# Which heads ScalarE's score pair takes, and one first pass over two PSUM banks on VectorE

## The chip, the cores and the metric

The kernel runs on one core of a Trainium2 chip. A core has five engines with instruction queues of their own: TensorE (PE in the profile; PEld is its weight load), VectorE (DVE), ScalarE (ACT), GpSimd (POOL) and SyncE (SP), which issues most DMAs. The metric is the device time of one execution in microseconds, as the median of several runs. Before the change it is 758.08 us, the median of 6 runs between 755.37 and 759.51.

## The reference

Two independent branches are computed from two inputs of 2048 rows and 640 columns, and their results stand side by side in the output.

```python
# A: spectral filter
X = rfft2(x);  y = irfft2(X * (w_r + 1j * w_i))           # to bf16
# B: attention, 32 heads of width 20
q, k, v = split(x @ wqkv)
p = softmax(q @ k.T * 20 ** -0.5)                         # 2048 x 2048 for each head
y = (p @ v) @ wo
out = concatenate([A, B], axis=-1)
```

The softmax has 32 x 2048 x 2048 exponentials. They are the bulk of the work outside TensorE.

## The kernel before, in words

**Units and tiles.** The attention is cut into 32 units. A unit is one block of 512 queries (`qc`) for a group `g` of four heads. The four heads sit on four groups of 32 partitions, so that their score matmuls use four separate row groups of TensorE. A unit has 16 key tiles `kt` of 128 keys, and for each key tile four heads `j` (0 to 3): 64 score tiles of 128 x 512, 2048 in all. A score tile is one matmul (`score_mm`, line 816) into one PSUM bank.

**Two ways to an exponential.** ScalarE takes two tiles at once. They lie in banks 0 and 1, or in 2 and 3, by turns; one activation of 128 x 1024 (`try_exp`, line 1413) writes their exponentials in f16 into a ring of 14 slots, that is seven pairs. VectorE takes the four heads of one key tile, a quad, and approximates the exponential by integer arithmetic. Each of the four tiles gets a first pass out of its PSUM bank into a quarter of a buffer `Ib` (`dve_fill`, line 950). When all four are there, two more passes over 2048 columns follow (lines 992 and 993), and a small scaling of V (line 1000). There are two buffers, hence at most two quads under way.

**PV.** A wave of four matmuls, one for each head of one key tile (`try_pv`, line 1071), multiplies exponentials with V. A key tile of ScalarE's needs one wave and a quad of VectorE's needs three, since its approximation is a sum of three parts. A wave is issued only when all four heads of the key tile are there. With eight tiles waiting (`VMIN`) the planner issues two waves together, under pressure from the ring also one.

**Banks.** Banks 4 to 7 (`POOLB`) are for everything but ScalarE's pairs: VectorE's tiles, the PV sum of the unit, and the jobs of projections, of the filter branch and of the output.

**The order.** The order of every engine's instructions is written when the kernel is built, by a planner (`run`) that keeps a time for each engine, a cost for each instruction and the moment from which each result is visible. It takes steps as engines come free: `try_exp` for ScalarE, `pick_dve` for VectorE, `step_pe` for TensorE. The latter first tries `try_act_fill`, then PV waves, then a job of the other branch, then a fill for VectorE alone (`try_dve_fill`), and at last a filler matmul [...] (line 1502). Nothing is decided at run time; the chip only keeps the order on each engine and the waits between engines.

**Picking.** `try_act_fill` needs a free pair of banks. `pick_set` fills ScalarE's pair with two tiles of different heads: first from `aq`, the open tiles of a key tile that ScalarE has begun, then from the next key tile. `pick_dve_tile` offers a tile for the same group of matmuls from `dq`, the open tiles of VectorE's quad, if its head isn't among those of the group:

```python
for t in self.dq:
    if t[2] not in bad_j and all(t[2] != d[0][2] for d in dts):
        return t
```

`dve_wants` allows it while VectorE's queued work is under 2.0 us (1.6 us with 0.6 us counted for a second tile), and while fewer than three of the four banks are held by others than PV. `free_bank` takes the lowest free bank of `POOLB`. At most three first passes are in flight (`MAXD`).

Of the kernel before, what the change touches and what calls it, by code (L numbers as in the profile page):

```python
# [297 lines left out]
class KB:  # L298
# [449 lines left out]
    def start_attention(self):  # L748
        self.rem = [[(kt, j) for kt in range(16) for j in range(4)] for _ in range(NU)]
        self.ua = 0  # L750
        self.qs = [list(range(16)) for _ in range(NU)]
        self.aq = []
        self.dq = []
        self.grp = 0
        self.sets = []
        self.act_started = False
        self.pn = 0
        self.dbatch = 0
        self.dtiles = []
        self.dfly = 0  # L760
        self.batches_open = {}
        self.bat = {}
        self.pv = []
        self.upv = 0
        self.pv_bank = {}
        self.pv_started = {}
        self.pv_left = [64] * NU
        self.units_done = 0
        self.act_tiles = 0
        self.dve_tiles = 0  # L770
        self.alias_done = set()
# [80 lines left out]
    DMIN = 14  # L852
    DMIN_LAST = 12

    def free_bank(self):
        for b in self.POOLB:
            if self.bank_owner[b] is None and self.P.peek("pe", w=[("ps", b)]) <= self.now:
                return b
        return None
# [4 lines left out]
    def try_act_fill(self):  # L864
        if self.ua >= NU:
            return False
        banks = self.SETS[self.grp]
        if any(self.bank_owner[b] is not None for b in banks):
            return False
        if len(self.sets) >= 2:  # L870
            return False
        if self.P.peek("pe", w=[("ps", b) for b in banks]) > self.now:
            return False
        tiles = self.pick_set(len(banks))
        if not tiles:
            return False
        left = sum(4 * len(q) for q in self.qs[self.ua:self.ua + 2]) + len(self.aq)
        if len(tiles) < len(banks) and left > len(tiles) and self.act_started and not self.starved():
            return False
        for t in tiles:  # L880
            self.take_tile(t)
        bl = banks[:len(tiles)]
        rk = set()
        for u, kt, j in tiles:
            rk.update(self.kq_keys(u, kt))
        dts = []
        while len(tiles) + len(dts) < 4 and self.dve_wants(len(dts)):
            db = self.free_bank()
            if db is None:
                break  # L890
            dt = self.pick_dve_tile(set(t[2] for t in tiles), dts)
            if dt is None:
                break
            dts.append((dt, db))
            self.dve_take(dt, db)
        wk = [("ps", b) for b in bl]

        def fn(e):
            inst = None
            for (u, kt, j), b in zip(tiles, bl):  # L900
                inst = self.score_mm(e, u, kt, j, b)
            return inst
        n = len(tiles)
        self.put("pe", fn, 216.0 + 4.0 * (n - 1), r=list(rk), w=wk, name="fillA", mode="S")
        for b in bl:
            self.bank_owner[b] = "act"
        self.sets.append((tiles, bl, self.grp))
        self.grp ^= 1
        self.act_started = True
        self.act_tiles += n  # L910
        for dt, db in dts:
            self.dve_fill(dt, db, 4.0)
        return True

    def starved(self):
# [20 lines left out]
        self.dfly += 1  # L936
        self.dve_tiles += 1

    def dve_fill(self, t, bank, occ):
        u, kt, j = t  # L940
        self.put("pe", lambda e: self.score_mm(e, u, kt, j, bank), occ, r=self.kq_keys(u, kt), w=[("ps", bank)], name="fillD", mode="S")
        b = self.dbatch % 2
        i = len(self.dtiles)
        self.dtiles.append(t)
        I16_ = self.Ib[b].bitcast(I16)
        o = I16_[:, i * 512:(i + 1) * 512]
        in_ = self.ps[:, bank, :]

        def fn(e, en):
            return e.tensor_scalar(o, in_, 0.0, 31744.0, ALU.max, ALU.min)  # L950
        al = self.first("xn3", ("xz", 3)) if b == 1 else []

        bt = self.bat.setdefault(self.dbatch, [0, None])

        def done():
            self.bank_owner[bank] = None
            self.dfly -= 1
            bt[0] += 1
            if bt[1] is not None and bt[0] == bt[1][0]:
                bt[1][1]()  # L960
        self.dve_push([(fn, 604.0, [("ps", bank)], [("I", b, i)] + al, [], "p1")], done)
        if len(self.dtiles) == 4:
            self.close_batch()

# [492 lines left out]
    def try_dve_fill(self, room):  # L1457
        if not self.act_started or self.ua >= NU or room < 216.0 + (2 if self.mode != "S" else 1) * self.SW or self.dve_backlog() > self.DVE_LOW:
            return False
        dts = []  # L1460
        used = set()
        while len(dts) < 2 and self.dve_wants(len(dts)):
            db = self.free_bank()
            if db is None:
                break
            dt = self.pick_dve_tile(used, dts)
            if dt is None:
                break
            dts.append((dt, db))
            self.dve_take(dt, db)  # L1470
        for i, (dt, db) in enumerate(dts):
            self.dve_fill(dt, db, 216.0 if i == 0 else 4.0)
        self.nown += len(dts)
        return bool(dts)

# [752 lines left out]
```

## Time and profile before

| | us |
|---|---|
| median of 6 runs | 758.08 |
| the profiled execution | 756.85 |
| its span, first to last instruction | 755.0 |
| ScalarE busy (784 of 797 instructions are exponentials) | 729.5 |
| VectorE busy | 672.4 |
| TensorE busy, its ends modelled | 723.5 |
| GpSimd busy | 133.5 |

A row of groups reads: line, engine and operation, what is written and read with its size, how often, then total busy time and mean length in ns, then the engine's idle time just before these instructions and what ended it. Successive instructions of one engine overlap a little: the exponentials are 1.120 us long by the row and start 0.904 us apart (the median). A line of the timeline reads: start, length, engine, line, operation, how many instructions it merges, and in brackets the idle time before it and who ended that.

### The profile page before, as it was taken

The numbers are of one execution on the slowest core, as the hardware profiler recorded it, in microseconds if no ns is written. First come the engines' busy times: TensorE is split into PE (matmuls) and PEld (weight loads), VectorE is DVE, ScalarE is ACT, GpSimd is POOL, SyncE is SP. The second block draws the span as 40 slices with busy tenths as digits, with TensorE's granted clock in tenths as the row PEclk, the third lists the DMA queues.
The fourth block names the chain that finished last, engine by engine and source line by source line (L and its number), as shares of the span: only waits on it lengthen the run. The fifth ranks groups of instructions, "written<-read, shape, count | busy, mean of one in ns | idle before, by whom it ended". The sixth has DMA issues, their size and how long they took to land.

```text
span 755.0 us, 16333 instructions
## 1 busy us (share of the span) xinstructions
PE 723.5 (96%) x6488; PEld 231.7 (31%) x6537; DVE 672.4 (89%) x1259; ACT 729.5 (97%) x797; POOL 133.5 (18%) x141
## 2 busy tenths in 40 slices
PE   8999999999999999999999999999999999999997
PEld 4422332423322222232233333322322333333233
DVE  3599999989899998999998899999898998898995
ACT  5899999999999999999999999999999999999995
POOL 7398740000000100003020022000000000000000
PEclk9999999999999999999999999999999999999999
DMA  9022321102012126113020121130010211111101
GB/s 307 26 68 89 104 95 40 44 8 62 21 38 55 49 78 205 43 47 116 19 52 7 56 54 35 36 98 22 20 47 19 88 36 55 39 52 43 43 13 38
DMA packets 43502, 44.66 MB, mean 59 GB/s; under 512 B 16740, under 2 KB 36582, under 8 KB 43166
## 3 DMA queue, kind: packets, MB, share of 16 engines
q1 hardware_dynamic: 42654, 42.25, 19.0%
q0 software_dynamic: 768, 1.32, 0.7%
q8 instruction: 53, 0.87, 0.5%
q14 instruction: 27, 0.22, 0.1%
HBM read 28.47 MB, written 8.36 MB: 49 GB/s over the span
## 4 chain that ended last, share of the span: by engine, by line
ACT 68%; PE 23%; DVE 8%; issue 1%; DVEq 0%
ACT arena L1413 67%; PE ps L816 8%; PE ps L1071 5%; DVE arena L950 3%; PE ps L1821 2%; PE ps L649 2%; PE ps L698 2%; PE ps L620 1%; PE ps L1217 1%; DVE arena L993 1%; DVE arena L992 1%; DVE arena L1853 1%; DVE arena L1000 1%; PE ps L1977 1%; PE ps L578 1%
## 5 line engine op out<-in xcount | busy, mean ns | idle before, releaser
L1413 ACT ACTIVATE arena<-ps 128x1024 f16<-128x1024 f32 x784 | 722.3, 1120 | 8.5 <-PE ps L816 7.2
L950 DVE TENSOR_SCALAR arena<-ps 128x512 int16<-128x512 f32 x480 | 320.3, 682 | 32.8 <-PE ps L816 29.5
L816 PE MATMUL ps<-arena 32*128 32x512 bf16 x2048 | 308.9, 385 | 12.7 <-ACT arena L1413 8.5
L1071 PE MATMUL ps<-arena 128*32 128x512 f16 x3008 | 235.7, 385 | 1.9 <-DVE arena L1000 1.0
L816 PEld LDWEIGHTS ps<-arena 32*128 32x128 bf16 x2048 | 76.0, 91 | 292.2 <-ACT arena L1413 270.6
L1123 POOL TENSOR_TENSOR arena<-arena 128x512 bf16<-128x512 f32 x30 | 41.3, 1376 | 510.2 <-DMA arena<-rd 510.2
L992 DVE TENSOR_SCALAR arena<-arena 128x2048 int16<-128x2048 int16 x120 | 88.5, 738 | 3.8 <-PE ps L1071 3.4
L993 DVE TENSOR_SCALAR arena<-arena 128x2048 int16<-128x2048 int16 x120 | 86.2, 718 | 0.6
L1071 PEld LDWEIGHTS ps<-arena 128*32 128x32 bf16 x3008 | 50.9, 94 | 96.0 <-issue 64.3
L649 PE MATMUL ps<-arena 128*128 128x512 bf16 x148 | 44.4, 383 | 2.7 <-issue 1.9
L1821 PE MATMUL ps<-arena 128*128 128x322 bf16 (+1 forms) x198 | 38.2, 304 | 0.8 <-DVE arena L950 0.6
L1977 PE MATMUL ps<-arena 128*128 128x320 bf16 (+1 forms) x192 | 35.7, 302 | 0.0
L698 PE MATMUL ps<-arena 128*128 128x160 bf16 x320 | 31.5, 234 | 1.3 <-DVE arena L950 0.5
L1853 DVE TENSOR_TENSOR arena<-ps,arena 128x644 bf16<-128x644 f32 (+1 forms) x34 | 27.9, 821 | 3.2 <-PE ps L1821 2.8
L1925 PE MATMUL ps<-arena 128*128 128x512 bf16 (+3 forms) x122 | 29.2, 332 | 1.5 <-issue 1.4
L1000 DVE TENSOR_SCALAR arena<-arena 128x96 bf16<-128x96 bf16 x120 | 29.8, 249 | 0.0
L1217 PE MATMUL ps<-arena 128*128 128x320 bf16 (+1 forms) x152 | 28.8, 302 | 0.6 <-DVE arena L950 0.6
L698 PEld LDWEIGHTS ps<-arena 128*128 128x128 bf16 x320 | 21.3, 98 | 14.5 <-issue 9.8
L1102 DVE COPY arena<-ps 128x512 f32<-128x512 f32 (+1 forms) x33 | 21.9, 667 | 2.6 <-PE ps L1071 2.5
L661 DVE TENSOR_SCALAR arena<-ps 128x512 bf16<-128x512 f32 x34 | 23.2, 681 | 0.7 <-PE ps L649 0.6
L1738 PE MATMUL ps<-arena 128*128 128x512 bf16 x70 | 21.4, 383 | 1.6 <-issue 1.3
L704 DVE CAST arena<-ps 128x320 bf16<-128x320 f32 x32 | 15.5, 486 | 7.4 <-PE ps L698 7.2
(82 smaller groups left out, 367.9 us busy)
## 6 DMA issues: line engine op xcount, KB each, us to landing
arena<-rd SPq DMA_DIRECT2D x120, 64.0 KB
out_dram<-arena SPq DMA_DIRECT2D x32, 160.0 KB
arena<-in_A_x_dram SPq DMA_DIRECT2D x16, 160.0 KB
xs<-arena SPq DMA_DIRECT2D x16, 160.0 KB
arena<-xs SPq DMA_DIRECT2D x4, 640.0 KB
arena<-arena SPq DMA_DIRECT2D x105, 20.0 KB
arena<-ct SPq DMA_DIRECT2D x2, 1024.0 KB
arena<-ct SPq DMA_DIRECT2D x4, 512.0 KB
```

The lines of the kernel that those rows point to most:

```text
L649: return lambda e: e.matmul(o, l, r_, start=(cc == 0), stop=(cc == 4))
L698: return lambda e: e.matmul(o, l, r_, start=st, stop=(c == 4), skip_group_check=True)
L816: return e.matmul(self.ps[:, bank, :], self.KT[32 * j:32 * j + 32, g, kt * 128:(kt + 1) * 128], self.QT[32 * j:32 * j + 32, g, qc * 512:(q ...
L950: return e.tensor_scalar(o, in_, 0.0, 31744.0, ALU.max, ALU.min)
L992: self.dve_push([(lambda e, en: e.tensor_scalar(Ii, Ii, SH2, 0.0, ALU.subtract, ALU.max), occ, ik + pk, ik, [], "p3")], lambda: push(self. ...
L993: ops = [(lambda e, en: e.tensor_scalar(Gi, Ii, SH1, 0.0, ALU.subtract, ALU.max), occ, ik, [("G", b)], [], "p2")]
L1000: self.dve_push([(lambda e, en: e.tensor_scalar(vs, vi, W1, None, ALU.mult), 105.0, [("V", g // 2, kt), ("Vone",), ("Vpad",)], vk, [], "vs ...
L1071: inst = e.matmul(self.ps[32 * j:32 * j + 32, bank, :], v_, p_, start=s_, stop=False, tile_position=(0, 32 * j), skip_group_check=True)
L1123: self.pool_op(lambda e: e.tensor_tensor(on, of, bc, ALU.mult), 1600.0, r=pk + [("bcu", u, j) for j in range(4)] + [("bc", j) for j in ran ...
L1413: self.put("act", lambda e: e.activation(o, in_, AF.Exp, bias=ACT_BIAS, scale=ACT_SCALE), 0.8333 * 512 * n + 60.0, r=[("ps", b) for b in b ...
L1821: return lambda e: e.matmul(o, lhs, r_, start=st, stop=sp)
L1977: return lambda e: e.matmul(o, l, r_, start=(n == 0), stop=(n == 5))
```

## The change

The diff has two parts. In `try_act_fill`, after ScalarE's pair was picked in the old way, and if VectorE's quad has open tiles (`dq`) and VectorE wants work, the pair is picked again with the heads of the first two open tiles excluded, or else the head of the first. The new pair is used if it is complete and if it and the open tiles of ScalarE belong to at most two key tiles together. The second part concerns fills that carry two tiles for VectorE. `free_bank` gets an argument and prefers a bank that has a free neighbour, or, for the second tile, one that lies beside the first. If the two banks are neighbours, the first `dve_fill` only issues its matmul and notes itself in `half`; the second one pushes a single first pass of 128 x 1024 over both banks, with a planned cost of 1137 in place of 2 x 604. Both banks are given back when this pass is done. `try_dve_fill` gets the same treatment.

```diff
+    def free_bank(self, near=None):
+        bs = self.POOLB
+        if near is not None:
+            ok = [b for b in bs if self.bank_owner[b] is None and self.P.peek("pe", w=[("ps", b)]) <= self.now]
+            bs = sorted(bs, key=lambda b: not any(abs(b - c) == 1 for c in (near or ok)))
+        for b in bs:
...
         tiles = self.pick_set(len(banks))
         if not tiles:
             return False
+        if self.dq and self.dve_wants(0):
+            for k in (2, 1):
+                alt = self.pick_set(len(banks), [t[2] for t in self.dq[:k]])
+                if len(alt) == len(banks) and len({t[:2] for t in self.aq + alt}) <= 2:
+                    tiles = alt
+                    break
...
-            db = self.free_bank()
+            db = self.free_bank([d[1] for d in dts])
...
-        for dt, db in dts:
-            self.dve_fill(dt, db, 4.0)
+        if len(dts) == 2 and abs(dts[0][1] - dts[1][1]) == 1:
+            if dts[0][1] > dts[1][1]:
+                dts = [(dts[0][0], dts[1][1]), (dts[1][0], dts[0][1])]
+            self.dve_fill(dts[0][0], dts[0][1], 4.0, True)
+            self.dve_fill(dts[1][0], dts[1][1], 4.0)
+        else:
+            for dt, db in dts:
+                self.dve_fill(dt, db, 4.0)
...
-    def dve_fill(self, t, bank, occ):
+    def dve_fill(self, t, bank, occ, first=False):
...
-        in_ = self.ps[:, bank, :]
+        half = self.half
+        self.half = (i, bank) if first else None
+        banks = [bank] if half is None else [half[1], bank]
+        i0 = i + 1 - len(banks)
...
+        o = I16_[:, i0 * 512:(i + 1) * 512]
+        in_ = self.ps[:, banks[0]:bank + 1, :].rearrange("p b n -> p (b n)")
...
+        if not first:
+            self.dve_push([(fn, 604.0 if half is None else 1137.0, [("ps", b_) for b_ in banks], [("I", b, i0 + q) for q in range(len(banks))] + al, [], "p1")], done)
```

More of the change, by code (lines that the diff above doesn't have):

```diff
@@ L758, in start_attention @@
         self.dbatch = 0
+        self.half = None
         self.dtiles = []
@@ L853 @@
     DMIN_LAST = 12
-    def free_bank(self):
-        for b in self.POOLB:
+    def free_bank(self, near=None):
[4 more added lines that the diff above has]
+        for b in bs:
             if self.bank_owner[b] is None and self.P.peek("pe", w=[("ps", b)]) <= self.now:
@@ L945, in dve_fill @@
         I16_ = self.Ib[b].bitcast(I16)
-        o = I16_[:, i * 512:(i + 1) * 512]
-        in_ = self.ps[:, bank, :]
+        half = self.half
+        self.half = (i, bank) if first else None
+        banks = [bank] if half is None else [half[1], bank]
+        i0 = i + 1 - len(banks)
+        assert half is None or half == (i - 1, bank - 1)
+        o = I16_[:, i0 * 512:(i + 1) * 512]
+        in_ = self.ps[:, banks[0]:bank + 1, :].rearrange("p b n -> p (b n)")
         def fn(e, en):
@@ L955, in done @@
         def done():
-            self.bank_owner[bank] = None
-            self.dfly -= 1
-            bt[0] += 1
+            for b_ in banks:
+                self.bank_owner[b_] = None
+                self.dfly -= 1
+                bt[0] += 1
             if bt[1] is not None and bt[0] == bt[1][0]:
                 bt[1][1]()
-        self.dve_push([(fn, 604.0, [("ps", bank)], [("I", b, i)] + al, [], "p1")], done)
+        if not first:
+            self.dve_push([(fn, 604.0 if half is None else 1137.0, [("ps", b_) for b_ in banks], [("I", b, i0 + q) for q in range(len(banks))] + al, [], "p1")], done)
         if len(self.dtiles) == 4:
@@ L1462, in try_dve_fill @@
         while len(dts) < 2 and self.dve_wants(len(dts)):
-            db = self.free_bank()
+            db = self.free_bank([d[1] for d in dts])
             if db is None:
@@ L1470, in try_dve_fill @@
             self.dve_take(dt, db)
+        two = len(dts) == 2 and abs(dts[0][1] - dts[1][1]) == 1
+        if two and dts[0][1] > dts[1][1]:
+            dts = [(dts[0][0], dts[1][1]), (dts[1][0], dts[0][1])]
         for i, (dt, db) in enumerate(dts):
-            self.dve_fill(dt, db, 216.0 if i == 0 else 4.0)
+            self.dve_fill(dt, db, 216.0 if i == 0 else 4.0, two and i == 0)
         self.nown += len(dts)
```

## The prediction

> **What bounds the kernel now.** First the page: shares by engine, then the chain that ended last.
>
> ```profile
> span 755.0 us, 16333 instructions
> ...
> PE 723.5 (96%) x6488; PEld 231.7 (31%) x6537; DVE 672.4 (89%) x1259; ACT 729.5 (97%) x797; POOL 133.5 (18%) x141
> ...
> ACT 68%; PE 23%; DVE 8%; issue 1%; DVEq 0%
> ```
>
> ScalarE carries the chain. TensorE's 96% is modelled and not its ceiling: 44 of its matmuls (16.2 us) are the filler of line 1502, issued when the planner has nothing else. Next, the groups by line.
>
> ```profile
> L1413 ACT ACTIVATE arena<-ps 128x1024 f16<-128x1024 f32 x784 | 722.3, 1120 | 8.5 <-PE ps L816 7.2
> L950 DVE TENSOR_SCALAR arena<-ps 128x512 int16<-128x512 f32 x480 | 320.3, 682 | 32.8 <-PE ps L816 29.5
> ...
> L992 DVE TENSOR_SCALAR arena<-arena 128x2048 int16<-128x2048 int16 x120 | 88.5, 738 | 3.8 <-PE ps L1071 3.4
> L993 DVE TENSOR_SCALAR arena<-arena 128x2048 int16<-128x2048 int16 x120 | 86.2, 718 | 0.6
> ```
>
> 784 exponentials take two score tiles each (1568), 480 first passes one each: together the 2048 of the problem. In the timeline the first exponential starts at 13.0 us, the last ends at 743.3, and 11.7 us follow. Of the 783 steps from one start to the next, 732 are 0.911 us in the mean; the other 51 are over 1.0 us and hold 15.7 us more than 0.911 each. So time falls in one way: VectorE takes more quads of four tiles, each of which removes two exponentials, 2 x 0.911 = 1.82 us. VectorE must find the time, and from 40 to 700 us it has 54 us idle. The list of waits names the largest reason, first passes waiting for TensorE's scores; the timeline shows how:
>
> ```profile
> DVE arena L950 <- PE ps L816: 29.5, 61, 1.5
> ```
>
> ```profile
> 527.66 0.39 PE L816 MATMUL ps<-arena 32*128 32x512 bf16 x2
> ...
> 528.36 0.18 DVE L1000 TENSOR_SCALAR arena<-arena 128x96 bf16<-128x96 bf16 x1
> ...
> 528.53 0.39 PE L816 MATMUL ps<-arena 32*128 32x512 bf16 x2
> ...
> 529.40 0.39 PE L816 MATMUL ps<-arena 32*128 32x512 bf16 x3
> ...
> 529.87 0.69 DVE L950 TENSOR_SCALAR arena<-ps 128x512 int16<-128x512 f32 x1 [1.33 <-PE ps L816]
> ```
>
> "x2" is ScalarE's pair alone, "x3" carries one tile for VectorE. At 527.66 no bank was free. At 528.53 one was, but VectorE's last open tile was head 3 and ScalarE's pair was heads 2 and 3; it had to wait for 529.40, and VectorE stood for 1.33 us.
>
> I sorted all 784 groups by the state that the planner itself keeps when it writes them (counts, no times): 424 carry one VectorE tile, 23 two, and 337 none. Of these 337, 146 found no free bank, 91 had enough queued or three banks held, 40 could open no quad, and **60 had a bank and an open tile but only clashing heads**. Setting the 480 passes of that order against the trace's 480, 75 waits over 0.09 us hold 31.1 us: 27 waits with **17.4 us** come after a clash, 24 with 8.2 us after "no free bank", the rest hold 5.5 us.
>
> **What the Trainium skill says.** *Vector Engine (DVE) Microarchitecture Reference*, section 5.2, gives one- and two-source operations 1.0417 ns a column plus about 75 ns an instruction after overlap. The trace agrees: in runs of first passes, starts are 0.601 us apart (median), 512 columns are 0.533, so the fixed part is 0.068. *TensorEngine Tiling (Array Packing)*, "Restrictions and Gotchas", says that different row tiles write to different PSUM banks: heads sit on four row groups, so one group holds four tiles at most, one per head and bank. The trace's x4 group takes 0.40 us against 0.39 for x2, so a VectorE tile riding along is nearly free. *PSUM — Partial Sum Buffer*, "PSUM bank collisions", asks for a guard by bank: a pass over two banks frees neither until it ends. No row of before shows such a pass.
>
> **The change part by part.**
>
> *Pair choice.* While a VectorE quad has open tiles and VectorE wants work, ScalarE's pair avoids the heads of the next two, or else of the next one. Nothing is added to any queue; the same matmuls and exponentials come in another order. Among the 500 groups with an open tile and a wish for one, the old pair already avoids both heads in 245, so about 255 picks change, far more than the 60 that clash. What can be won: 17.4 us of VectorE idleness at most, 0 at least. Some of these waits will meet the bank limit instead (146 against 60 groups). I take 12, about 70%.
>
> *One pass over two banks.* It removes a first pass and makes the other 1024 wide. Bound per merge: at least 0.047 us saved (the slope from the 644-wide row of line 1853, 0.744 apart, gives (0.744 - 0.601)/132 = 1.083 ns a column; 0.601 - 512 x 0.00108), at most 0.092 (slope from the 320-wide row of line 704, 0.410 apart). I take 0.07. How often: before, 26 fills take two tiles for VectorE (23 with a pair, 3 without), 18 of them on neighbouring banks. Of the 500 groups only 102 saw two or more banks free. With the preference for neighbours and fewer clashes I estimate 40 merges, between 15 and 100: 2.8 us, from 0.7 to 9. Its price is a bank held up to 0.6 us longer (one first pass), with three or four banks left for everything but ScalarE's pairs; PV and filter jobs queue for it. At 40 merges I put this at nothing because of the 44 filler matmuls; uncovered it is 40 x 0.5 = 20 us of bank time in 4 x 730, under 1%.
>
> *Sum.* VectorE gains 12 + 2.8 = 14.8 us. A quad costs it 4 x 0.601 + 0.599 + 0.602 + 0.220 (starts apart of lines 950, 992, 993, 1000) = 3.83 us, and shortens the time in which it can work by 1.82. So 14.8 / (3.83 + 1.82) = 2.6 quads, 5.2 exponentials, **4.7 us**. TensorE pays two more PV waves per quad: an x12 run takes 0.83 against 0.62 for x8, so 2.6 x 2 x 0.21 = 1.1 us, hidden by the filler matmuls and otherwise lost from the gain. The DMA queues see the same transfers. Next late, once the clashes are gone, are banks. The profiled execution took 756.85, 1.85 more than its span, and the median of runs is 1.23 above it. So span 750.3, profiled 752.2, median 758.1 - 4.7 = 753.4.
>
> **Rivals.**
>
> *Late PV waves, slower.* A PV wave needs the four heads of one key tile. Now ScalarE takes heads 0-1, then 2-3, so every key tile is complete in two groups; with 255 changed picks many take three or four. The ring holds seven pairs. If a slot isn't read when it comes round, the exponential waits and everything behind it on ScalarE too. Such gaps cost 15.7 / 51 = 0.31 us each today. Sixteen more use up the gain, 24 make it slower by 0.3%; that is one in ten of the changed picks. At one in seven (36): +11.2 - 4.7 = 6.5, median 764.6. For it: ScalarE has no other slack. Against: today a key tile's last pair has about five groups until reuse, and two thirds of PV runs take two waves, so the planner can still go to single ones.
>
> *Banks decide, no change.* The 60 freed groups find VectorE served a group earlier, then short of a bank. R falls to some 3 us: 0.5 quad, 1 us, 757. For it: 146 groups without a bank. Against: the clashing groups had one, by definition.
>
> *A larger gain.* All 31.1 us of waits go and 100 merges come: 31.1 + 7 = 38 us, 6.7 quads, 12.3 us, 745.8. Against: 8.2 us of this is lack of banks.
>
> *The merging hardly happens* (below 20): it takes 1.4 us from VectorE's gain, 0.5 from the forecast; that lies inside it.
>
> **How the numbers follow.** Faster by 2 to 8 us 0.43 (own range 750 to 756), larger gain 0.13, within 2.3 us 0.19, slower by late waves or a worse order of the filter's work 0.25. 0.3% of 758 is 2.3 us, about what a measurement of this kernel can tell. Hence faster 0.56, same 0.19, slower 0.25. The range leaves out about half of the large gain (0.06) and half of the slower case (0.13): 747 to 763.5. Its lower end also covers the upper bounds (17.4 + 9 = 26.4 us, 8.5 us, 749.6), its upper end a plan that loses a quad or two by its order.
>
> **What would show it.** Right: 775 to 781 exponentials and 122 to 124 quads; VectorE's wait for line 816 down from 29.5 to below 20 us; more x4 groups than 26; 20 to 60 passes of 1024 columns at about 1.13 us apart. Wrong: 784 or more exponentials; ScalarE steps over 1.0 us well above 51, ended by PV; many more single-wave PV runs; the wait for line 816 unchanged, or moved to lines 992 and 1228; a longer end than 11.7 us after the last exponential.

## The result and the profile after

The changed kernel takes 759.78 us (median of 35 runs, 756.18 to 766.62) against 758.0 us for the kernel before, run beside it (72 runs). The ratio is 1.0026, with a 95% interval from 1.0014 to 1.0038: about 2 us slower, where the forecast was 4.7 us faster. The mean granted TensorE clock was 0.998 or more in 25 of the 37 executions whose clock is on record, with a median of 758.76 us, and lower in the other 12, with 763.79. The profiled execution took 761.03 us with a span of 759.2, so it lies 1.25 us above its median, and that of before 1.2 below. The two profiles are therefore 4.2 us apart where the medians are 1.8, and what is counted in them below explains the 4.2.

The page of the changed kernel, its shares and its chain; line 1437 is now the exponential, 972 the first pass, 817 the scores, 1095 PV.

```profile
span 759.2 us, 16357 instructions
...
PE 722.0 (95%) x6507; PEld 232.7 (31%) x6556; DVE 681.8 (90%) x1269; ACT 727.2 (96%) x791; POOL 133.5 (18%) x141
...
ACT 43%; PE 41%; DVE 12%; issue 2%; DMA 1%; SPq 0%
```

ScalarE has less to do than before (727.2 against 729.5 us), yet its share of the chain fell from 68% to 43%, and TensorE's rose from 23% to 41%. ScalarE now waits for TensorE more often. The shares alone do not say that this is bad, though: `heads_k1` below, one of the two fastest kernels of this study, has nearly the same ones:

```profile
ACT 46%; PE 40%; DVE 12%; issue 1%; DVEq 0%
```

The groups by line, each shape apart:

```profile
L1437 ACT ACTIVATE arena<-ps 128x1024 f16<-128x1024 f32 x778 | 720.0, 1100 | 14.5 <-PE ps L817 9.1 <-PE ps L1095 4.2
L972 DVE TENSOR_SCALAR arena<-ps 128x512 int16<-128x512 f32 x470 | 313.6, 681 | 28.0 <-PE ps L817 26.1
...
L1016 DVE TENSOR_SCALAR arena<-arena 128x2048 int16<-128x2048 int16 x123 | 92.9, 757 | 5.9 <-PE ps L1095 5.5
...
L972 DVE TENSOR_SCALAR arena<-ps 128x1024 int16<-128x1024 f32 x11 | 13.4, 1222 | 4.5 <-PE ps L817 4.3
```

VectorE took 123 quads, three more, and ScalarE 778 exponentials, six fewer, as many as the forecast had. The wide pass was used 11 times. New is the "PE ps L1095 4.2" behind the exponential: ScalarE stands for PV. An exponential writes into a ring slot, and has to wait until PV has read what lay there. The list of waits for ScalarE, before and after:

```profile
ACT arena L1413 <- PE ps L816: 7.2, 13, 2.3
...
ACT arena L1413 <- PE ps L1071: 0.3, 1, 0.3
```

```profile
ACT arena L1437 <- PE ps L817: 9.1, 16, 2.3
...
ACT arena L1437 <- PE ps L1095: 4.2, 14, 0.6
```

This list counts only idle time behind the end of a row, and an exponential's row (1.1 us) outlasts the step to the next one (0.904, the median). So I took the span apart along ScalarE's starts: time to the first exponential; each exponential at 0.904; what steps up to 1.0 us have above 0.904; what longer steps have above 0.904, by the line that released them last (scores or PV); and what follows the last one. The terms add up to the span.

| us | first start | exponentials | x 0.904 | short steps | long, scores (count) | long, PV (count) | after | span |
|---|---|---|---|---|---|---|---|---|
| before | 13.0 | 784 | 708.7 | 5.2 | 14.2 (45) | 1.9 (6) | 12.0 | 755.0 |
| changed | 12.8 | 778 | 703.3 | 5.1 | 17.2 (52) | 8.0 (20) | 12.8 | 759.2 |

The six exponentials gave 5.4 us. The long steps took 9.1 back, 6.1 of it in waits for PV and 3.0 in waits for scores, and the end 0.8. The waits for PV alone are more than the exponentials gave. The rest, 3.8 us, is of the size that a change of order without any purpose makes (last experiment).

### The profile page after: what moved, and what is told of

The parts are those of the page before. It is cut to its first block, busy times and chain, and to the rows that moved or that the text cites. A ratio compares the mean times of both kernels' runs of the same rounds, so it can differ in the third digit from the quotient of the medians.

```text
span 759.2 us, 16357 instructions
## 1 busy us (share of the span) xinstructions
PE 722.0 (95%) x6507; PEld 232.7 (31%) x6556; DVE 681.8 (90%) x1269; ACT 727.2 (96%) x791; POOL 133.5 (18%) x141
## 4 chain that ended last, share of the span: by engine, by line
ACT 43%; PE 41%; DVE 12%; issue 2%; DMA 1%; SPq 0%
ACT arena L1437 43%; PE ps L817 14%; PE ps L1095 10%; DVE arena L972 5%; PE ps L1848 3%; PE ps L649 3%; DVE arena L1016 2%; PE ps L698 2%; PE ps L2004 2%; DVE arena L1017 2%; PE ps L1241 2%; PE ps L1765 2%; PE ps L620 2%; PE ps L1952 1%; DVE arena L1024 1%
## 5 line engine op out<-in xcount | busy, mean ns | idle before, releaser
L972 DVE TENSOR_SCALAR arena<-ps 128x512 int16<-128x512 f32 (+1 forms) x481 | 326.8, 694 | 32.4 <-PE ps L817 30.5
L817 PE MATMUL ps<-arena 32*128 32x512 bf16 x2048 | 306.6, 384 | 14.2 <-ACT arena L1437 9.9
L1095 PE MATMUL ps<-arena 128*32 128x512 f16 x3032 | 239.2, 385 | 5.7 <-DVE arena L1017 2.5
L1016 DVE TENSOR_SCALAR arena<-arena 128x2048 int16<-128x2048 int16 x123 | 92.9, 757 | 5.9 <-PE ps L1095 5.5
L1017 DVE TENSOR_SCALAR arena<-arena 128x2048 int16<-128x2048 int16 x123 | 89.6, 729 | 0.7
L1095 PEld LDWEIGHTS ps<-arena 128*32 128x32 bf16 x3032 | 52.2, 94 | 104.9 <-issue 67.9
L1952 PE MATMUL ps<-arena 128*128 128x512 bf16 (+3 forms) x121 | 29.5, 332 | 2.1 <-issue 1.0
L1024 DVE TENSOR_SCALAR arena<-arena 128x96 bf16<-128x96 bf16 x123 | 28.2, 230 | 0.0
```

What stands on the lines that cost most here:

```text
L817: return e.matmul(self.ps[:, bank, :], self.KT[32 * j:32 * j + 32, g, kt * 128:(kt + 1) * 128], self.QT[32 * j:32 * j + 32, g, qc * 512:(q ...
L1016: self.dve_push([(lambda e, en: e.tensor_scalar(Ii, Ii, SH2, 0.0, ALU.subtract, ALU.max), occ, ik + pk, ik, [], "p3")], lambda: push(self. ...
L1017: ops = [(lambda e, en: e.tensor_scalar(Gi, Ii, SH1, 0.0, ALU.subtract, ALU.max), occ, ik, [("G", b)], [], "p2")]
L1095: inst = e.matmul(self.ps[32 * j:32 * j + 32, bank, :], v_, p_, start=s_, stop=False, tile_position=(0, 32 * j), skip_group_check=True)
```

## The experiments

Three theories, of which the expectations speak. *Ring*: the new pairs are drawn from two key tiles, so a key tile takes longer to complete, its PV wave is later, and exponentials wait for ring slots. *Bank*: the wide pass, and the lack of banks, took the gain. *Order*: any change gives the planner another order of the filter's and the output's work, which moves the time without a mechanism of its own. Every kernel below computes the same function; the order, the number of tiles that VectorE takes and the form of its first pass differ, and in two of them the length of the ring. The order that each kernel writes out gives a count that matters here: in how many successive groups a key tile of ScalarE's is completed. Before, all 392 take two groups. In the changed kernel 84 take two, 153 three, 121 four and 31 five, and 328 of 778 pairs are mixed from two key tiles. Quads, exponentials and mixed pairs can be counted in this written order before a kernel runs, so they test no theory where an expectation below has them; the waits and the time do.

The kernel before ran beside each group of experiments, with a median of 759.05 us for the next two parts, 757.85 for the third and 756.92 for the fourth. The ratios are to these, and are to be compared rather than the times.

### Each part alone

`heads` is the pair choice without the rest, `merge` the wide pass without the pair choice:

```diff
# heads: in try_act_fill only; free_bank, dve_fill and try_dve_fill as before
+        if self.dq and self.dve_wants(0):
+            for k in (2, 1):
...
# merge: the changed kernel without these lines
```

> The pair choice alone, first passes stay 512 wide. Ring theory (mixed pairs complete a key tile later, so exponentials wait for ring slots that PV hasn't read): the cost comes from this part, so ScalarE steps over 1.0 us ended by PV stay near the 20 of the changed kernel (6 before), with some 8 us; quads are at least 123. The time then lies within 0.3% of the changed kernel, 757 to 762. Bank theory (the wide pass and the banks it holds took the gain): without it the quads stay above 120 and the time falls to 752 to 755.

> The wide pass alone, ScalarE's pair is picked as before. Ring theory: every key tile is again complete in two groups, ring waits fall back to about 6 steps and 2 us; the time is that of the kernel before within 0.3% (756 to 760), since a dozen or two merges are worth 1 to 2 us of VectorE. Bank theory: the loss comes from here, 760 to 763, with fewer quads than 120.

| | median us | ratio (95% interval) | quads | exponentials x 0.904 | long, scores | long, PV | after | span |
|---|---|---|---|---|---|---|---|---|
| heads | 763.54 | 1.0058 (1.0041 to 1.0075) | 124 | 701.5 | 17.1 (49) | 8.8 (21) | 11.7 | 759.3 |
| merge | 762.32 | 1.0042 (1.0025 to 1.0059) | 119 | 710.5 | 15.3 (44) | 2.9 (4) | 11.3 | 759.5 |

This table and those below leave out the first start and the short steps. `heads` and `merge` also have 1.9 and 1.7 us in long steps that the trace puts down to neither scores nor PV (1.5 and 1.3 to a matmul of the filter, the rest to nothing). The waits of ScalarE for PV in the two, from the list of waits (line 1077 is PV in `heads`, 1089 in `merge`):

```profile
ACT arena L1419 <- PE ps L1077: 4.3, 12, 0.8
```

```profile
ACT arena L1431 <- PE ps L1089: 1.8, 1, 1.8
```

The waits for PV come with the pair choice and without the wide pass: 21 steps with 8.8 us, as in the changed kernel. The merge alone has 4. So far the ring theory holds, but not to the end: the merge alone loses too, which it doesn't explain, and `heads` was 763.54 us in the median against 757 to 762 expected. 1.2 us of its loss lie behind the last instruction: `heads` takes 3.0 us longer than its span (median of its executions), the kernel before 1.8. Its trace has a last transfer of the instruction queue that ends 3.6 us after the span; in the kernel before it is 0.7. The bank theory expected `heads` at 752 to 755; that is wrong by 8 us. Of the merge's 4.4 us of longer span, 1.8 stand in the number of quads, one fewer, and 1.7 in the waits put down to neither; the runs with a nudge, below, say more.

### A shorter ring

```diff
-    RING = 14
+    RING = 12
```

> The kernel before with a ring of six pairs instead of seven. Ring theory: a key tile complete in two groups has slack, so little changes: PV-ended steps up from 6 to about 8 to 12, time 758 to 762. Bank theory says nothing special: a smaller ring costs the same 0 to 4 us here as in the changed kernel.

> The changed kernel with a ring of six pairs. Ring theory: the slack is used up by the mixed pairs, so PV-ended steps multiply (20 to 60 or more) and the time rises by 10 to 20 us, to 770 to 780. Bank theory: the same 0 to 4 us as the kernel before loses with six pairs, 760 to 764.

Six pairs in place of seven made the kernel before 757.39 us (0.9978, 0.9966 to 0.999), no loss at all and a little under the 758 to 762 expected, and the changed kernel 775.36 us (1.0227, 1.0185 to 1.0268). The groups by line of the latter, the exponential's row, and the lists of waits for ScalarE of the latter and then of the former:

```profile
L1437 ACT ACTIVATE arena<-ps 128x1024 f16<-128x1024 f32 x772 | 718.2, 1082 | 30.7 <-PE ps L1095 22.3 <-PE ps L817 7.1
```

```profile
ACT arena L1437 <- PE ps L1095: 22.3, 59, 1.2
```

```profile
ACT arena L1413 <- PE ps L1071: 1.3, 4, 0.5
```

Long steps ended by PV are 79 with 35.1 us, against 8 with 2.8 us in the kernel before with the same short ring. One slot pair decides nothing where every key tile is complete in two groups, and 15 us where most take three to five, although the changed kernel with the short ring takes three more quads (126). That is the ring theory's own dose: the bank theory expected 760 to 764, and no change of order in this study moves the time by nearly as much.

A single wait shows the steps. It is taken from the changed kernel's timeline:

```profile
161.62 1.02 ACT L1437 ACTIVATE arena<-ps 128x1024 f16<-128x1024 f32 x1
...
162.55 0.12 PEld L1095 LDWEIGHTS ps<-arena 128*32 128x32 bf16 x8 [0.23 <-issue]
162.56 0.62 PE L1095 MATMUL ps<-arena 128*32 128x512 f16 x8
163.10 0.09 PEld L817 LDWEIGHTS ps<-arena 32*128 32x128 bf16 x2 [0.42 <-ACT arena L1437]
...
163.22 1.94 ACT L1437 ACTIVATE arena<-ps 128x1024 f16<-128x1024 f32 x2 [0.59 <-PE ps L1095]
```

The exponential at 163.22 is the 153rd. Its slots were last written by the 146th, seven earlier, with head 2 of key tile 9 and head 0 of key tile 10. The order has heads 0, 1, 3 and 2 of key tile 10 in the 146th, 147th, 148th and 150th pair. So the wave could not be issued before the 150th had been computed, at 160.4. It runs at 162.56, two waves in one go, while ScalarE already stands: its step is 1.60 us. The mixing is not all of this wait: in the 2.1 us between, the order gives TensorE scores and projections first (among them 0.59 us of line 649 at 161.71).

### Fewer mixed pairs

`heads_clash` picks again only if every open tile of VectorE's quad clashes with the old pair; `clash` does the same with the wide pass left in. `heads_k1` avoids the head of the first open tile alone. `whole` is the changed kernel with pairs from one key tile only:

```diff
# heads_clash, clash
-        if self.dq and self.dve_wants(0):
+        if self.dq and self.dve_wants(0) and {t[2] for t in self.dq} <= {t[2] for t in tiles}:
# heads_k1
-            for k in (2, 1):
+            for k in (1,):
# whole
-                if len(alt) == len(banks) and len({t[:2] for t in self.aq + alt}) <= 2:
+                if len(alt) == len(banks) and len({t[:2] for t in alt}) == 1 and len({t[:2] for t in self.aq + alt}) <= 2:
```

> First passes stay 512 wide; ScalarE's pair is picked again only where the old pick clashes with every open tile of VectorE's quad. 115 pairs are mixed from two key tiles in place of 333, and 258 of 388 key tiles are complete in two groups in place of 71 of 388. Ring theory: the quads stay at 124 (776 exponentials, 7.2 us less than before), PV-ended steps fall from 21 to about 6 to 9 with 2 to 4 us, and the time is 751 to 756, clear of the kernel before. Bank theory (a changed pick only moves VectorE's waits): 758 to 762 as with the full pair choice.

> First passes stay 512 wide; the pair avoids only the head of the first open tile. 220 pairs mixed, 181 of 387 key tiles complete in two groups. Ring theory: between the two, 8 to 12 PV-ended steps with 3 to 5 us, 774 exponentials (9 us less than before), 752 to 757. Bank theory: 758 to 762.

> The changed kernel, wide passes included, but a re-picked pair must come from one key tile, so no pair is mixed and 336 of 392 key tiles are complete in two groups. Ring theory: PV-ended steps fall from 20 to about 5 with 2 us. It also has fewer picks to help VectorE with: 120 quads and 784 exponentials as before. Time that of the kernel before within 0.4%, 756 to 761. Bank theory: 760 or more, because the wide passes stay.

> The changed kernel, wide passes included, re-picking only on a clash. 100 pairs mixed. Ring theory: about 9 PV-ended steps with 3 us, 776 exponentials; 754 to 759, with up to 4 us more after the last exponential than before, by the order of the output's work. Bank theory: 760 or more.

| | median us | ratio (95% interval) | mixed pairs | quads | long, scores | long, PV | after | span |
|---|---|---|---|---|---|---|---|---|
| heads_clash | 753.44 | 0.9945 (0.9928 to 0.9962) | 115 | 124 | 12.8 (42) | 3.3 (6) | 14.1 | 749.4 |
| heads_k1 | 752.57 | 0.9931 (0.9908 to 0.9954) | 220 | 125 | 13.0 (37) | 2.9 (8) | 16.2 | 750.1 |
| whole | 757.08 | 0.9989 (0.9976 to 1.0003) | 0 | 120 | 13.1 (36) | 1.7 (5) | 12.9 | 755.4 |
| clash | 759.79 | 1.0022 (1.0008 to 1.0036) | 100 | 124 | 16.0 (46) | 4.8 (9) | 16.6 | 758.1 |

With as many quads as `heads` or one more, `heads_clash` and `heads_k1` lose most of the waits for PV and are 4.4 and 5.3 us faster than the kernel before beside them. The granted clock does not make this gain: half of the executions of the kernel before were below 0.998, but against those at 0.998 or more, at the same clock, the two are still 3.1 and 4.3 us faster. The groups by line of `heads_k1` (exponential 1419, first pass 956, scores 816, PV 1077) show both sides of it:

```profile
L1419 ACT ACTIVATE arena<-ps 128x1024 f16<-128x1024 f32 x774 | 713.1, 1108 | 8.3 <-PE ps L816 6.3 <-PE ps L1077 0.8
L956 DVE TENSOR_SCALAR arena<-ps 128x512 int16<-128x512 f32 x500 | 332.8, 682 | 19.7 <-PE ps L816 17.2
```

Five more quads than before, ten fewer exponentials (9.0 us), PV behind ScalarE's idle time at 0.8 us, and VectorE's wait for scores down to 17.2 us from 29.5. It is the forecast's mechanism, at twice the forecast's saving in exponentials (9.0 against 4.7 us), though 4.2 us of it are lost again after the last exponential.

`whole` has 13 wide passes and no mixed pairs, and is level with the kernel before; so wide passes need not cost anything. `clash` missed its expectation: it has the quads (124) and 9 waits for PV in place of 20, and yet 759.79 us. It has only two wide passes. The profiles of `clash` and `heads_clash` are 8.7 us apart in span (the medians 6.4): 3.2 in waits for scores, 1.5 for PV, 2.5 after the last exponential, 1.0 before the first, 0.5 in short steps. Another 1.0 us lies behind the last instruction, as in `heads`. Two passes of about 1.1 us can hardly do that directly; what else differs is the order. The next part shows how far an order alone can move the time; that it did so here is inferred, not shown.

### A nudge without a mechanism

```diff
# null602 and null606: the kernel before; k1_606: heads_k1; the pass on the chip is the same
-        self.dve_push([(fn, 604.0, ...
+        self.dve_push([(fn, 602.0, ...        # or 606.0
# merge1208: merge
-        604.0 if half is None else 1137.0
+        604.0 if half is None else 1208.0
```

> The kernel before, with the first pass entered in the planner at 602 in place of 604 (the chip's instruction is the same). Order theory (any nudge reorders the filter's and the output's work and moves the time by some tenths of a per cent without a mechanism): 480 passes, time between 754 and 762, by more than 0.1% off the kernel before. Theory of the wide pass (the wide pass itself costs what the merge alone lost): the nudge leaves the time within 0.1%, 757 to 759.

> The same with 606 in place of 604. Order theory: 754 to 762 and unlike the sister run by more than 0.1%. Theory of the wide pass: within 0.1% of the kernel before and of the sister run.

> The wide pass alone, but the planner books it at twice 604, so its order takes no advantage of it. Theory of the wide pass: the loss of the merge alone stays, 761 to 764, since the passes on the chip are as wide and hold the banks as long. Order theory: the time moves by some tenths of a per cent either way from the 762.3 of the merge alone, 757 to 765, with the number of quads (119 there) setting most of it.

> The pair choice that avoids one head, first passes 512 wide, with the planner's nudge of 606. If its gain is one of mechanism (fewer clashes without the ring waits), it survives the nudge: 751 to 756, 776 to 778 exponentials, PV-ended steps at most 10. If it was luck of the order, the time returns to 757 to 760.

| | median us | ratio (95% interval) | quads | long, scores | long, PV | span |
|---|---|---|---|---|---|---|
| null602 | 761.53 | 1.0055 (1.0036 to 1.0074) | 120 | 17.7 (54) | 3.2 (6) | 759.8 |
| null606 | 755.35 | 0.9974 (0.9962 to 0.9987) | 120 | 11.8 (39) | 1.2 (3) | 752.5 |
| merge1208 | 759.61 | 1.0038 (1.0024 to 1.0052) | 118 | 13.9 (48) | 1.7 (5) | 759.5 |
| k1_606 | 752.53 | 0.9943 (0.9927 to 0.9959) | 123 | 11.2 (38) | 2.6 (7) | 750.7 |

A cost that the planner books 0.3% lower or higher, with the same instructions on the chip, makes the kernel 0.55% slower or 0.26% faster. The quads are the same; what moves is mostly ScalarE's wait for scores, 17.7 or 11.8 us. The groups by line of the two, the exponential's row of `null602` and then of `null606`:

```profile
L1413 ACT ACTIVATE arena<-ps 128x1024 f16<-128x1024 f32 x784 | 723.5, 1119 | 11.6 <-PE ps L816 8.6 <-PE ps L1071 2.0
```

```profile
L1413 ACT ACTIVATE arena<-ps 128x1024 f16<-128x1024 f32 x784 | 721.4, 1114 | 6.8 <-PE ps L816 5.8 <-PE ps L1071 0.5
```

So a difference of 2 us between two versions of this kernel, in one order each, is inside what a meaningless nudge does; this goes for the changed kernel's 0.26% too. What lies outside is what repeats: the 20, 21 and 79 waits for PV with the full pair choice against 3 to 9 in every other kernel, and the gain of the milder pair choice in `heads_clash`, `heads_k1` and `k1_606` (0.9931 to 0.9945). The fourth kernel with a milder choice, `clash`, does not have the gain, so it repeats in three orders of four.

Whether the wide pass costs a quad by itself stays open. `merge1208` at 759.61 us lies below the 761 to 764 expected from the wide pass, but the kernel before beside it was faster too: in ratio it loses as much as `merge` did (1.0038 and 1.0042), so it does not tell the two theories apart. A quad or two were lost in both kernels that have the wide pass alone (119 and 118 against 120 in both nudged ones), none in `whole`, and the saving of a pass is real but small; two orders are too few to tell.

## Why the prediction was wrong

*Quads and exponentials: the count came true, in part by luck.* 2.6 more quads and 5.2 exponentials less were forecast, 4.7 us; measured 3, 6 and 5.4 us. But the time for them did not come from where it was forecast:

*Where VectorE's time was to come from: wrong.* The clashes went as foreseen. With the passes sorted as in the prediction, waits after a clash fell from 27 with 17.4 us to 4 with 1.6. But those after "no free bank" rose from 24 with 8.2 us to 51 with 24.7. I had taken 70% of the 17.4 us as won and left the rest to the bank limit, but the limit took all of it; the list of waits has 30.5 us where it had 29.5:

```profile
DVE arena L972 <- PE ps L817: 30.5, 65, 1.0
```

VectorE has its three more quads by other means: 4.2 us of longer span and 5 us less idle time in all (77.4 against 82.6 us), most of it before other instructions than the first passes. The rival "banks decide" had the place right and the effect on the quads wrong. In `heads_k1` the bank waits are 12.0 us, so their size is not a fixed price of solving the clashes; but they exceed the 8.2 us of before in every kernel that solves them (19.4 us in `k1_606`). That banks hold VectorE there is read from the order, and was not tested by a run of its own.

*"Nothing is added to any queue; the same matmuls and exponentials come in another order": the step that failed.* I counted 255 changed picks against 60 useful ones, and priced the others at nothing. They mix pairs, and ScalarE then waits for ring slots: 14 further long steps ended by PV, with 6.1 us, more than the 5.4 that the exponentials gave. The rival of late PV waves had the mechanism and nearly the size: 0.31 us for each further step and 24 of them for a loss of 0.3%; it came to fewer and longer ones, 0.44 us each. Seven more long steps with 3.0 us wait for scores; these are not shown to come from the pair choice, since `null602` has 3.5 us more of them than before with nothing changed. I gave the rival only 0.25, a worse order of other work included, because a key tile's last pair had "about five groups until reuse". That was slack for a key tile complete in two groups, the state before; the order after mostly takes three to five, and I did not carry that through. The short ring showed how near the edge that is. With the milder choices the waits for PV stay at 2.6 to 3.3 us without wide passes, and the gain is there.

*The wide pass: small, as said.* It saves 2 x 0.601 - 1.138 = 0.064 us (starts apart after a wide pass, medians of three kernels, 1.133 to 1.140), within the bounds of 0.047 to 0.092 and near the 0.07 taken. There were 11, below the 15 that I had as the least: the groups that carry two tiles for VectorE did not become more but fewer, 19 against 23 (449 carry one). It is not the pair choice that did this, since `merge` without it has 19 and 11 too. Eleven passes save 0.7 us of VectorE, not 2.8.

*The range held the time, the sign did not.* "A worse order of the filter's work" stood in the slower case without a price. The two nudged kernels give one: 0.55% slower and 0.26% faster. So the lost gain is explained by the waits for PV; that the changed kernel ends 2 us slower rather than level is within the price of an order and has no cause shown.

## What to carry to other kernels

When a pick is changed to help one engine, count how many picks change besides those that had to: each of the others moves the completion of something that a buffer waits for. A ring with slack for the order of today may have none for a freer one; shortening it by one step is a cheap run that tells whether the slack is used up. With an order written by a planner, nudge one cost by a third of a per cent first, in both directions, and take differences below what that does for noise unless the waits behind them repeat. A count that comes true is no proof of the way to it: look at the wait that was to go.

## What the runs showed that I had not expected

A ring of six pairs is as fast as one of seven for the kernel before (0.9978), so 2 KB a partition can be had for something else there. The best pair choice of the study avoids one head instead of two, without wide passes: 752.57 us against 757.85 beside it, ratio 0.9931, and 0.9943 with the nudge.
